# Four channels beside each other instead of two in the state of an FFT convolution

## The chip, the cores and the metric

The kernel runs on one core of one Trainium2 chip. The metric is the device time of one execution in microseconds; the time before is the median of three runs.

## The reference

A Hyena filter (a long convolution over the sequence) is followed by a feed-forward block with a cosine gate. Cut to what matters:

```python
# x, v: (4, 12480, 128); pos_emb: (12480, 64); w1: (64, 64); w2: (64, 128)
h_filt = (np.maximum(pos_emb @ w1, 0.0) @ w2) * np.exp(-0.01 * pos)[:, None]
u = x * v
L = 2 * S
Uf = np.fft.rfft(u, n=L, axis=1)
Hf = np.fft.rfft(h_filt, n=L, axis=0)
y = np.fft.irfft(Uf * Hf[None], n=L, axis=1)[:, :S]
x = (x * y).reshape(B * S, D)              # 49920 tokens of 128
h = x @ w_in                               # w_in: (128, 2048)
out = (h * np.cos(h)) @ w_out              # w_out: (2048, 128)
```

All of it is float32.

## The kernel before

The convolution is done by transforms written as matmuls. The sequence of one batch is seen as a grid of N1 = 96 by N2 = 120, and four transforms follow one another, each over one of the two sides of the grid:

- `f1` (lines 413 to 446 and 576): for each pair of channels, one matmul for each channel with the channel's data as weights (`u[:, b, 0:KE, i]`) and the table `c1` as the moving operand (192 columns).
- `f2` (449 to 483): for each of 96 frequencies, the table `w` as weights and the state of all 128 channels as the moving operand, 256 columns (real and imaginary part). `f2_product` multiplies with the filter's spectrum `h` on VectorE and adds on GpSimd.
- `i1` (485 to 498): again one channel at a time, the channel's data as weights, table `cs` as the moving operand (120 columns).
- `i2` (500 to 521): for each of 120 positions, a table `tm` as weights and the state of all channels as the moving operand (128 columns). The result times `x` goes to DRAM as rows for the feed-forward block.

The state between the transforms lies in one SBUF tile, `slots`, and every transform writes its result back into it. The 128 channels are 64 pairs: index `b` counts the pairs (`CB` = 64), index `i` the two of a pair. In each partition `slots` has, for each pair, 240 places with the two floats of the pair beside each other:

```python
slots = spool.tile([P, CB, 2 * N2, 2], F32, name="slots")
parts = slots[:, :, 0:2 * N1, :].rearrange("p b (r k) i -> p r k b i", r=2)
above = slots[:, :, 2 * N1:2 * N2, :]
```

So a transform that reads all channels at one place (f2, i2) takes pieces of two floats, 8 bytes, 1920 bytes apart. A transform that reads one channel (f1, i1) takes single floats 8 bytes apart. A step that writes one pair (the evictions of f1 and i1) writes a contiguous row. `ftile` holds the filter in the same manner, with 144 places for a pair (pieces 1152 bytes apart).

The program first makes the filter (lines 314 to 376), transforms it and the first batch (`f1`, then `f2` of both together), and runs `i1` of the first batch. In this first part (up to 348 us) a matmul is issued over all its weight columns at once. From `i2` of the first batch on, the convolution is issued beside the feed-forward block: a loop over blocks of tokens and 16 chunks of the hidden width issues one chunk at a time and takes as many steps of the convolution with it as a count of steps owed says. `tiled[0]` is then set, and `mm` (line 129) issues each matmul as two: one for output rows 0 to 63, one for the rest, each with its own weights and with the same moving operand. The order on every engine is the order of the program text; nothing is scheduled by costs.

In the feed-forward block a chunk is an up-projection (`ph`, 512 columns), the gate on ScalarE and VectorE, sums on GpSimd, and down-projections (`acca`, `accb`, 128 columns, line 787). Each batch passes f1, f2, i1 and i2 in turn; `i2` of one batch runs together with the loads and products of the next (`u_sums`, line 406).

Of the kernel before, what the change touches and what calls it, by code (L numbers as in the profile page):

```python
# [17 lines left out]
P = 128  # L18
# [15 lines left out]
def kernel(  # L34
# [62 lines left out]
    KF = N1 - 2 * (N2 - N1)  # L97
    CB = D // 2
    assert R * N2 == S and S + TAPS - 1 <= 2 * M and math.exp(DECAY * TAPS) < 2.0 ** -150
    assert D == P and DFF % P == 0 and FO * 2 == P and N1 % 2 == 0 and R <= P  # L100
# [11 lines left out]
    dram = ctx.enter_context(tc.tile_pool(name="dram", bufs=1, space=DRAM))  # L112
    hd = dram.tile([N1 // 2, N2, 2, CB, 4], F32, name="hd")
    zd = dram.tile([NROWS, G, D], F32, name="zd")
# [240 lines left out]
    def filter_hidden(bank, aT, i, peT, w1_sb):  # L355

        pa = bank()
        nc.tensor.matmul(pa[:, 0:ROWS * H], w1_sb[:, :], peT[:, :], start=True, stop=True)
        nc.scalar.activation(aT[:, 0:H, i * ROWS:(i + 1) * ROWS],
                             pa[:, 0:ROWS * H].rearrange("p (n a) -> p a n", a=H), AF.Relu)  # L360

    def filter_out(pool, bank, aT, slots, j, w2_sb):

        ps = bank()
        for i, jj in enumerate((j, H - 1 - j)):
            nc.tensor.matmul(ps[0:FR, i * 2 * D:(i + 1) * 2 * D], aT[:, jj, 0:FR],
                             w2_sb[:, :], start=True, stop=True)
        above = pool.tile([FR, 2, CB, 2], F32, name="above", bufs=2)
        pj = ps[0:FR, :].rearrange("p (n b i) -> p n b i", n=4, i=2)
        nc.scalar.copy(out=above[:, :, :, :], in_=pj[:, 2:4])  # L370
        a = H - 2 - 2 * j
        for place, op in ((a, ALU.add), (ODD + a, ALU.subtract)):
            nc.vector.tensor_tensor(
                slots[0:FR, :, place:place + 2, :].transpose([0, 2, 1, 3]),
                pj[:, 1::-1], above[:, :, :, :], op=op)
# [14 lines left out]
    def clear_gap(u):  # L390

        nc.gpsimd.memset(u[:, :, H:ODD, :], 0.0)

# [12 lines left out]
    def u_sums(u, tiles, a, takers):  # L406
        both = tiles[0][:, :, :].rearrange("p h (n b i) -> p h n b i", n=UA, i=2)
        below, above = both[:, 0, ::-1, :, :], both[:, 1, :, :, :]
        for place, op, e in ((a, ALU.add, takers[0]), (ODD + a, ALU.subtract, takers[1])):
            e.tensor_tensor(u[0:R, :, place:place + UA, :].transpose([0, 2, 1, 3]),  # L410
                            below, above, op=op)


    def f1_mm(ps, u, b, i):

        mm(ps[0:KE, i * 2 * N1:(i + 1) * 2 * N1], u[:, b, 0:KE, i],
           c1[0:u.shape[0], :, :].rearrange("p r k -> p (r k)"))
# [10 lines left out]
    def f1_evict(ps, b, share):  # L428
        copy, negated = f1_takers(b, share)
        pj = ps[:, 0:4 * N1].rearrange("p (i r k) -> p r k i", i=2, r=2)  # L430
        copy(out=parts[0:ODD, :, :, b, :], in_=pj[0:ODD])  # L431
        yield
        copy(out=parts[ODD:KE, 0, :, b, :], in_=pj[ODD:KE, 1])  # L433
        negated(parts[ODD:KE, 1, :, b, :], pj[ODD:KE, 0])
        yield

    def f1_evict_filter(ps, b, share):

        copy, negated = f1_takers(b, share)
        pj = ps[:, 0:4 * N1].rearrange("p (i k) -> p k i", i=2)  # L440
        near, far = ftile[:, b, :, :], above[:, b, :, :]
        copy(out=near[0:ODD], in_=pj[0:ODD, 0:N1 + KF])
        copy(out=far[0:ODD], in_=pj[0:ODD, N1 + KF:])
        yield
        copy(out=near[ODD:KE, 0:N1], in_=pj[ODD:KE, N1:])
        negated(near[ODD:KE, N1:], pj[ODD:KE, 0:KF])
        negated(far[ODD:KE], pj[ODD:KE, KF:N1])
        yield

    def f2_mm(ps, w, k1, i, filt=False):  # L450


        k = k1 + i
        pi = ps[0:N2, :].rearrange("p (r b g i) -> p g r b i", r=2, g=2, i=2)[:, i]
        if not filt:
            mm(pi, w[:, i, :], parts[0:KE, :, k])
        elif k < KF:
            both = ftile[0:KE, :, k:k + N1 + 1:N1, :].rearrange("p b r i -> p r b i")
            nc.tensor.matmul(pi, w[:, i, :], both, start=True, stop=True)
        else:  # L460
            for r, src in enumerate((ftile[0:KE, :, k, :], above[0:KE, :, k - KF, :])):
                nc.tensor.matmul(pi[:, r], w[:, i, :], src, start=True, stop=True)

    def f2_product(pool, ps, h, k1, whole):


        y = parts[0:N2, :, k1:k1 + 2, :, :].rearrange("p r k b i -> p r b (k i)")
        t = pool.tile([N2, 2, CB, 4], F32, name="t", bufs=2)
        uu = ps[0:N2, :].rearrange("p (r b j) -> p r b j", r=2, j=4)
        if whole:  # L470
            for r, (dst, hh) in enumerate(((y, h[:, :, :, :]), (t[:, :, :, :], h[:, ::-1, :, :]))):
                u = uu[:, r]
                twice = bass.AP(tensor=u.tensor, offset=u.offset,
                                ap=[u.ap[0], [0, 2], *u.ap[1:]])
                nc.vector.tensor_tensor(dst, twice, hh, op=ALU.mult)
                yield
        for r, op in ((0, ALU.subtract), (1, ALU.add)):
            if not whole:
                nc.vector.tensor_tensor(y[:, r], uu[:, 0], h[:, r], op=ALU.mult)
                yield  # L480
                nc.vector.tensor_tensor(t[:, r], uu[:, 1], h[:, 1 - r], op=ALU.mult)  # L481
            nc.gpsimd.tensor_tensor(y[:, r], y[:, r], t[:, r], op=op)  # L482
            yield

    def i1_mm(ps, b, i):
        for r in range(2):
            n = max(N1, CB + CB // 2 + 1) if tiled[0] else N1
            mm(ps[0:n, (i * 2 + r) * N2:(i * 2 + r + 1) * N2],
               slots[0:N2, b, r * N1:r * N1 + n, i], cs[:, r, :])

    def i1_evict(pool, ps, b):
# [3 lines left out]
        for h, op in ((0, ALU.add), (1, ALU.subtract)):  # L495
            nc.vector.tensor_tensor(slots[0:N1, b, h * N2:(h + 1) * N2, :], pj[:, 0],
                                    other[:, :, :], op=op)
            yield

    def i2_mm(ps, t, g, part):  # L500
        for i in range(part * G // 2, (part + 1) * G // 2):
# [8 lines left out]
            for r, place in enumerate(places):  # L510
                mm(ps[0:R, i * D:(i + 1) * D], t[:, i, r, :], slots[0:N1, :, place, :],
                   start=(r == 0), stop=(r == 1))
# [83 lines left out]
    def f2_units(bank):  # L596
        with tc.tile_pool(name="there", bufs=3) as pool:
            ws, hs = {}, {}

            def before(j):  # L600
                ws[j] = pool.tile([KE, 2, N2], F32, name="w")
                nc.sync.dma_start(ws[j][:, :, :], wd[j, :, :, :])
                hs[j] = pool.tile([N2, 2, CB, 4], F32, name="h")
                nc.sync.dma_start(hs[j][:, :, :, :], hd[j, :, :, :, :])
# [10 lines left out]
    def f2_both_units(bank):  # L615

        with tc.tile_pool(name="both", bufs=2) as pool:
# [15 lines left out]
            def after(j, ps):  # L633
                h = pool.tile([N2, 2, CB, 4], F32, name="h", bufs=3)
                nc.scalar.activation(h[:, :, :, :].rearrange("p r b j -> p (r b j)"),
                                     ps[1][0:N2, :], AF.Copy, scale=1.0 / M)
# [58 lines left out]
    def inverse_units(bank, b):  # L695
# [3 lines left out]
        if b + 1 == B:  # L699
            yield from i2_units(bank, b, 3)  # L700
            return
        new = u_units(b + 1, 3, slots[0:R, :, :, :],
                      lambda j, half: nc.vector if half else nc.gpsimd,
# [9 lines left out]
    def forward_units(bank, back):  # L713

        f2 = f2_units(bank)
        next(f2)
        yield from f1_units(bank, slots[0:R, :, :, :])
        yield from f2
# [116 lines left out]
    with tc.manual_schedule():  # L835
        with tc.tile_pool(name="psum", bufs=8, space=PSUM) as psum, \
# [4 lines left out]
            spool = ctx.enter_context(tc.tile_pool(name="slots", bufs=1))  # L841
            slots = spool.tile([P, CB, 2 * N2, 2], F32, name="slots")
            parts = slots[:, :, 0:2 * N1, :].rearrange("p b (r k) i -> p r k b i", r=2)
            above = slots[:, :, 2 * N1:2 * N2, :]
            aT = above.rearrange("p b j i -> p b (j i)")

# [4 lines left out]
            with tc.tile_pool(name="layers", bufs=1, side="right") as pool:  # L851
# [8 lines left out]
                for i in range(1, NCH):  # L860
                    pes[i] = filter_load(pool, i)
                first_u = u_units(0, 3, slots[0:R, :, :, :],
                                  lambda j, half: nc.vector if half and j % 3 and j < 18
# [4 lines left out]
                window = filter_window(pool)  # L868
                nc.gpsimd.memset(aT[:, 0:H, NCH * ROWS:FR], 0.0)
                sines = forward_tables(pool)  # L870
# [15 lines left out]
            fpool = first.enter_context(tc.tile_pool(name="ftile", bufs=1, side="right"))  # L886
            ftile = fpool.tile([P, CB, N1 + KF, 2], F32, name="ftile")
            clear_gap(ftile[0:FR, :, :, :])
            with tc.tile_pool(name="out", bufs=1, side="right") as pool:
                for j in range(H // 2):  # L890
                    filter_out(pool, bank, aT, ftile, j, w2_sb)
                    for _ in range(1 + (j % 3 == 0)):
                        next(first_u)
            f1 = f1_units(bank, ftile[0:FR, :, :, :], 0.53, f1_evict_filter)
            for _ in first_u:
# [15 lines left out]
            def beside(units, pieces, factor, more=lambda pool: iter(())):  # L911
                with tc.tile_pool(name="convert", bufs=1) as pool:
# [8 lines left out]

            beside(f1_units(bank, slots[0:R, :, :, :], 0.55),
                   [(wind[:, c], w) for c, w in in_pieces], INV_TWO_PI)
# [124 lines left out]
```

## Time and profile before

| what | value |
|---|---|
| median of 3 runs | 3749.4 us (3748.94 to 3753.12) |
| profiled execution | 3748.55 us |
| its span, first to last instruction | 3746.8 us |
| mean granted TensorE clock | 0.994 |
| TensorE busy | 97% of the span |
| GpSimd, VectorE, ScalarE busy | 74%, 79%, 60% |

PE is TensorE's matmuls, PEld its weight loads, DVE VectorE, ACT ScalarE, POOL GpSimd. Each float32 matmul stands in the trace as two records. A name such as `cv<-slots,tm` says that `cv` (a PSUM tile; `ps` in the first part) is written from `slots` and `tm`; `96*64 96x128` is 96 rows by 64 columns of weights and a moving operand of 128 columns. The stages in the trace, from the first to the last matmul of each:

| batch | f1 | f2 | i1 | i2 |
|---|---|---|---|---|
| first, with the filter | 75 to 177 | 181 to 279 | 282 to 343 | 348 to 583 |
| second | 612 to 748 | 753 to 1084 | 1093 to 1201 | 1202 to 1424 |
| third | 1452 to 1586 | 1593 to 1921 | 1933 to 2074 | 2078 to 2300 |
| fourth | 2327 to 2464 | 2470 to 2798 | 2809 to 2950 | 2955 to 3089 |

After 3089 us only the feed-forward block is left.

### The profile page before, as it was taken

How to read it: one execution, taken by the hardware profiler on the slowest of the kernel's cores; microseconds unless marked ns; L12 is line 12 of the kernel's file. 1: busy time of each engine (PE TensorE's matmuls, PEld its weight loads, DVE VectorE, ACT ScalarE, POOL GpSimd, SP SyncE). 2: the span in 40 equal slices, each digit the busy share in tenths (PEclk: the TensorE clock that was granted, in tenths of full speed). 3: DMA queues.
4: the chain of work that ended last, by engine and by line, in shares of the span. 5: the costliest groups of instructions: out<-in, count | busy, mean ns of one | idle time of the engine just before them, and what ended most of it. 6: DMA issues, size and time to landing. Idle time of an engine off the chain costs nothing.

```text
span 3746.8 us, 101339 instructions
## 1 busy us (share of the span) xinstructions
PE 3631.1 (97%) x40298; PEld 2592.9 (69%) x40298; DVE 2962.2 (79%) x5812; ACT 2252.4 (60%) x4660; POOL 2786.1 (74%) x3271
## 2 busy tenths in 40 slices
PE   7898999999999999999999999999999999999999
PEld 6777776766668776666667776766667776666666
DVE  7887887788887777788877777788887667777777
ACT  5756666655554556655555555665555446666666
POOL 6667887588874887588874788578884447887877
PEclk9999999999999999999999999999999999999999
DMA  6263551022212661022210553012220350000000
GB/s 167 66 185 100 163 155 49 20 65 72 73 43 58 169 163 45 18 69 73 66 40 21 157 163 99 15 53 73 67 70 13 107 147 21 21 19 24 18 24 14
DMA packets 209710, 279.59 MB, mean 75 GB/s; under 512 B 17112, under 2 KB 146536, under 8 KB 209112
## 3 DMA queue, kind: packets, MB, share of 16 engines
q1 hardware_dynamic: 209239, 273.12, 25.7%
q8 instruction: 320, 5.24, 0.6%
q14 instruction: 151, 1.23, 0.1%
HBM read 193.64 MB, written 79.42 MB: 73 GB/s over the span
## 4 chain that ended last, share of the span: by engine, by line
PE 79%; DVE 7%; POOL 2%; ACT 2%; issue 1%; DMA 0%; ACTq 0%; SPq 0%; POOLq 0%; DVEq 0%
PE ph L132 28%; PE cv L132 20%; PE accb L787 16%; PE acca L787 12%; DVE gt L762 2%; DVE gt L756 2%; PE cv L136 1%; ACT gt L755 1%; PE ph L136 1%; POOL ts L770 1%; DVE slots L431 0%; ACT tile L818 0%; POOL slots L410 0%; POOL ts L773 0%; DVE slots L433 0%
## 5 line engine op out<-in xcount | busy, mean ns | idle before, releaser
L755 ACT ACTIVATE gt<-ph 128x512 int32<-128x512 f32 (+1 forms) x1374 | 818.5, 596 | 1175.2 <-PE ph L132 1123.3
L756 DVE SCALAR_TENSOR_TENSOR gt<-ph,gt 128x512 f32<-128x512 f32 (+1 forms) x1374 | 944.3, 687 | 676.8 <-ACT gt L755 666.8
L770 POOL TENSOR_TENSOR ts<-gt 128x512 f32<-128x512 f32 (+2 forms) x784 | 1005.0, 1282 | 608.7 <-PE accb L787 542.1
L132 PE MATMUL ph<-at,w_in_sb 128*64 128x512 f32 (+1 forms) x5496 | 1428.6, 593 | 26.6 <-ACT tile L818 17.0
L761 ACT ACTIVATE gt<-gt 128x512 f32<-128x512 f32 (+1 forms) x1568 | 972.2, 620 | 4.2 <-DVE gt L756 3.4
L762 DVE TENSOR_TENSOR gt<-ph,gt 128x512 f32<-128x512 f32 (+1 forms) x1374 | 932.3, 679 | 0.0
L787 PE MATMUL accb<-ts,w_out_sb 128*64 128x128 f32 (+2 forms) x9408 | 652.2, 272 | 0.0
L774 POOL TENSOR_TENSOR ts<-gt,ts 128x256 f32<-128x256 f32 (+2 forms) x784 | 574.3, 733 | 61.5
L773 POOL TENSOR_TENSOR ts<-ts,gt 128x256 f32<-128x256 f32 (+2 forms) x784 | 573.0, 731 | 61.5
L787 PEld LDWEIGHTS acca<-gt,w_out_sb 128*64 128x64 f32 x6272 | 404.5, 137 | 239.1 <-issue 200.2
L787 PEld LDWEIGHTS accb<-ts,w_out_sb 128*64 128x64 f32 x9408 | 546.1, 137 | 0.0
L787 PE MATMUL acca<-gt,w_out_sb 128*64 128x128 f32 (+2 forms) x6272 | 482.9, 272 | 0.0
L787 PEld LDWEIGHTS accb<-gt,w_out_sb 128*64 128x64 f32 x3136 | 230.1, 137 | 254.8 <-issue 198.3
L132 PEld LDWEIGHTS ph<-at,w_in_sb 128*64 128x64 f32 x5496 | 354.9, 137 | 51.3 <-ACT tile L818 22.4
L482 POOL TENSOR_TENSOR slots<-slots,t 120x256 f32<-120x256 f32 x384 | 281.3, 739 | 125.8 <-DVE t L481 81.3
L132 PEld LDWEIGHTS cv<-slots,tm 96*64 96x64 f32 (+1 forms) x3840 | 246.6, 128 | 129.0 <-issue 118.3
L787 PE MATMUL accb<-gt,w_out_sb 128*64 128x128 f32 (+1 forms) x3136 | 313.6, 273 | 5.1 <-DVE ot L808 3.3
L787 PE MATMUL acca<-ts,w_out_sb 128*64 128x128 f32 (+1 forms) x3136 | 311.6, 272 | 2.3 <-POOL ts L773 2.3
L132 PE MATMUL cv<-slots,tm 96*64 96x128 f32 (+1 forms) x3840 | 278.7, 287 | 7.4 <-POOL tm L306 5.6
L132 PEld LDWEIGHTS cv<-cs,slots 120*64 120x64 f32 (+1 forms) x3072 | 167.3, 125 | 80.3 <-issue 70.9
L787 PEld LDWEIGHTS acca<-ts,w_out_sb 128*64 128x64 f32 x3136 | 204.8, 137 | 3.1 <-POOL ts L773 2.8
L132 PEld LDWEIGHTS cv<-c,slots 104*64 104x64 f32 (+1 forms) x1536 | 118.3, 137 | 114.6 <-issue 63.6
(145 smaller groups left out, 4134.9 us busy)
## 6 DMA issues: line engine op xcount, KB each, us to landing
h<-hd SPq DMA_DIRECT2D x144, 240.0 KB
tm<-td SPq DMA_DIRECT2D x96, 312.0 KB
xt<-in_x_dram SPq DMA_DIRECT2D x120, 208.0 KB
vt<-in_v_dram SPq DMA_DIRECT2D x120, 208.0 KB
xs<-in_x_dram SPq DMA_DIRECT2D x120, 208.0 KB
zd<-xs SPq DMA_DIRECT2D x119, 208.0 KB
tile<-zd SPq DMA_DIRECT2D x96, 256.0 KB
w<-wd SPq DMA_DIRECT2D x144, 116.2 KB
```

The costliest lines, as they stand in the source:

```text
L132: nc.tensor.matmul(dst[lo:hi], left[:, lo:hi], right, start=start, stop=stop)
L136: nc.tensor.transpose(dst, src, ident[0:n, 0:n])
L482: nc.gpsimd.tensor_tensor(y[:, r], y[:, r], t[:, r], op=op)
L755: nc.scalar.activation(turns, ph[:, 0:m], AF.Identity, bias=phase)
L756: nc.vector.scalar_tensor_tensor(out=part, in0=ph[:, 0:m], scalar=phase, in1=turns, op0=ALU.add, op1=ALU.subtract)
L761: nc.scalar.activation(part, part, AF.Sin, scale=scale)
L762: nc.vector.tensor_tensor(part, ph, part, op=ALU.mult)
L770: nc.gpsimd.tensor_tensor(ts[:, 0:2, 0:half], gt[:, :, half:2 * half], gt[:, 0, 0:2 * half].rearrange("p (h n) -> p h n", h=2), op=ALU.sub ...
L773: nc.gpsimd.tensor_tensor(t[2], t[1], b11, op=ALU.add)
L774: nc.gpsimd.tensor_tensor(t[3], b21, t[2], op=ALU.subtract)
L787: nc.tensor.matmul(acc[h * CB:(h + 1) * CB, place, 0:r], w_out_sb[:, pair, weight, :], right[:, h * r:(h + 1) * r], start=(pair == 0 and i ...
```

## The change

The 64 pairs become 32 groups of four channels. `slots` gets the shape (128, 32, 240, 2, 2): a place holds the four floats of a group beside each other, `e` saying which pair of the group and `i` which of the pair, and channel pair `b` is now group `b // 2`, `e = b % 2`. All views follow. A transform that reads all channels at one place takes pieces of four floats, 16 bytes, 3840 bytes apart; one that reads one channel takes single floats 16 bytes apart; an eviction of one pair writes pieces of two floats at a pitch of 16 bytes. `ftile`, the filter's hidden layer `aT`, the spectrum `h` in DRAM (`hd`) and the product's term `t` are laid out in the same way. Each instruction computes on the same elements as before; only their addresses differ. The slots tile starts at a multiple of 16 bytes in both.

```diff
+    Q = CB // 2
-    hd = dram.tile([N1 // 2, N2, 2, CB, 4], F32, name="hd")
+    hd = dram.tile([N1 // 2, N2, 2, Q, 8], F32, name="hd")
...
 def u_sums(u, tiles, a, takers):
-            e.tensor_tensor(u[0:R, :, place:place + UA, :].transpose([0, 2, 1, 3]),
+            e.tensor_tensor(u[0:R, :, place:place + UA].rearrange("p c n e i -> p n c (e i)"),
                             below, above, op=op)
 def f1_mm(ps, u, b, i):
-        mm(ps[0:KE, i * 2 * N1:(i + 1) * 2 * N1], u[:, b, 0:KE, i],
+        mm(ps[0:KE, i * 2 * N1:(i + 1) * 2 * N1], u[:, b // 2, 0:KE, b % 2, i],
            c1[0:u.shape[0], :, :].rearrange("p r k -> p (r k)"))
 def f1_evict(ps, b, share):
-        copy(out=parts[0:ODD, :, :, b, :], in_=pj[0:ODD])
+        copy(out=parts[0:ODD, :, :, b // 2, b % 2, :], in_=pj[0:ODD])
...
 def f2_mm(ps, w, k1, i, filt=False):
-        pi = ps[0:N2, :].rearrange("p (r b g i) -> p g r b i", r=2, g=2, i=2)[:, i]
+        pi = ps[0:N2, :].rearrange("p (r c g j) -> p g r c j", r=2, g=2, j=4)[:, i]
-            mm(pi, w[:, i, :], parts[0:KE, :, k])
+            mm(pi, w[:, i, :], parts[0:KE, :, k].rearrange("p r c e i -> p r c (e i)"))
...
 def f2_product(pool, ps, h, k1, whole):
-        y = parts[0:N2, :, k1:k1 + 2, :, :].rearrange("p r k b i -> p r b (k i)")
-        t = pool.tile([N2, 2, CB, 4], F32, name="t", bufs=2)
+        y = parts[0:N2, :, k1:k1 + 2].rearrange("p r k c e i -> p r c (k e i)")
+        t = pool.tile([N2, 2, Q, 8], F32, name="t", bufs=2)
 def i1_mm(ps, b, i):
-               slots[0:N2, b, r * N1:r * N1 + n, i], cs[:, r, :])
+               slots[0:N2, b // 2, r * N1:r * N1 + n, b % 2, i], cs[:, r, :])
 def i1_evict(pool, ps, b):
-            nc.vector.tensor_tensor(slots[0:N1, b, h * N2:(h + 1) * N2, :], pj[:, 0],
+            nc.vector.tensor_tensor(slots[0:N1, b // 2, h * N2:(h + 1) * N2, b % 2, :], pj[:, 0],
                                     other[:, :, :], op=op)
 def i2_mm(ps, t, g, part):
-                mm(ps[0:R, i * D:(i + 1) * D], t[:, i, r, :], slots[0:N1, :, place, :],
+                mm(ps[0:R, i * D:(i + 1) * D], t[:, i, r, :], slots[0:N1, :, place].rearrange("p c e i -> p c (e i)"),
                    start=(r == 0), stop=(r == 1))
...
-            slots = spool.tile([P, CB, 2 * N2, 2], F32, name="slots")
-            parts = slots[:, :, 0:2 * N1, :].rearrange("p b (r k) i -> p r k b i", r=2)
+            slots = spool.tile([P, Q, 2 * N2, 2, 2], F32, name="slots")
+            parts = slots[:, :, 0:2 * N1].rearrange("p c (r k) e i -> p r k c e i", r=2)
```

## The prediction

> **What bounds the kernel now.** I read the busy shares first: TensorE is busy for 97% of the span. Since that may be a mean over stages with different limits, I then took the busy time of each engine by stage, with the borders at the first and last matmul of each stage of the convolution.
>
> ```profile
> PE 3631.1 (97%) x40298; PEld 2592.9 (69%) x40298; DVE 2962.2 (79%) x5812; ACT 2252.4 (60%) x4660; POOL 2786.1 (74%) x3271
> ```
>
> Columns by stage: window, its length, busy time of PE, PEld, DVE, ACT and POOL, granted clock, DMA share, GB/s.
>
> ```profile
> 75.50:176.60 101.10, 86.81 (x488) 81.73 (x487) 86.08 (x264) 79.92 (x283) 68.32 (x108) 0.95 0.24 71
> 282.30:343.10 60.80, 49.79 (x462) 46.95 (x462) 50.55 (x143) 40.19 (x124) 47.36 (x59) 0.92 0.21 62
> 348.10:582.90 234.80, 226.19 (x2752) 166.13 (x2750) 196.95 (x353) 158.27 (x336) 205.81 (x254) 0.99 0.53 155
> 1592.70:1920.90 328.20, 318.77 (x3337) 205.71 (x3336) 278.93 (x552) 192.91 (x352) 286.54 (x337) 1.00 0.24 69
> 1932.90:2074.10 141.20, 139.63 (x1960) 108.44 (x1956) 108.13 (x236) 75.59 (x173) 69.81 (x77) 1.00 0.07 20
> 2078.00:2300.00 222.00, 221.04 (x2706) 163.83 (x2704) 163.31 (x277) 117.95 (x216) 193.03 (x228) 1.00 0.60 163
> ```
>
> In order: the first transform of the filter and of batch 0, the third transform of batch 0, its fourth beside the feed-forward block, and second, third and fourth transform of a later batch. In the last three PE is busy for 97 to 99.6%, and the chain of waits there runs almost wholly over PE: what a matmul gains or loses goes into the span. In the first two PE has gaps.
>
> The third view is the timeline of PE, for the spacing from one group's start to the next group's. A pair is one record for each half of the columns, running side by side.
>
> ```profile
> 1596.29 0.65 PE L132 MATMUL cv<-slots,w 124*64 124x256 f32 x4
> 1596.75 0.41 PE L787 MATMUL accb<-gt,w_out_sb 128*64 128x128 f32 x4
> ...
> 2010.07 1.40 PE L132 MATMUL cv<-cs,slots 120*64 120x120 f32 x24
> 2011.30 0.61 PE L787 MATMUL acca<-gt,w_out_sb 128*64 128x128 f32 x8
> ...
> 2203.97 1.15 PE L132 MATMUL cv<-slots,tm 96*64 96x128 f32 x16
> 2204.94 0.62 PE L787 MATMUL acca<-gt,w_out_sb 128*64 128x128 f32 x8
> 2205.38 0.41 PE L787 MATMUL acca<-ts,w_out_sb 128*64 128x128 f32 x4
> ```
>
> The fourth transform takes 0.97/8 = 121 ns per pair of 128 columns where the feed-forward pair, with contiguous operands, takes 0.44/4 = 110. Over all groups of the trace the fourth transform has 122.5; the second has 243 per pair of 256 columns (230 in the group shown) where half of a contiguous 512-column pair (0.86/2, the ph groups) is 215. The third transform is at 1.23/12 = 102.5 for 120 columns: full rate. So there is an excess of 10 to 13%, only where the moving operand is read in pieces of 8 bytes and two halves run side by side: the second transform undivided (batch 0) has 218.
>
> The fourth view is the weight loads by shape; the mean is the second number behind the bar.
>
> ```profile
> L132 PEld LDWEIGHTS cv<-slots,tm 96*40 96x40 f32 x1920 | 223.9, 117 | 22.0 <-issue 22.0
> L132 PEld LDWEIGHTS cv<-cs,slots 120*64 120x64 f32 x1536 | 167.1, 138 | 78.8 <-issue 69.5 <-ACT ot L801 4.7 <-DVE slots L496 4.2
> L132 PEld LDWEIGHTS cv<-cs,slots 120*33 120x33 f32 x1536 | 159.2, 111 | 1.4 <-issue 1.4
> L366 PEld LDWEIGHTS ps<-w_sb,slots 128*96 128x96 f32 x120 | 19.5, 163 | 7.7 <-POOL ftile L392 1.5
> L462 PEld LDWEIGHTS ps<-slots,w 124*120 124x120 f32 x96 | 14.0, 180 | 0.0
> ```
>
> From 33 to 64 columns a load grows by 27 ns, 0.85 per column (40 to 64 from contiguous weights: 0.86; 96 contiguous: 163), so I read it as a fixed 84 ns, which the next matmul does not wait out (spacing 102.5, load 138), and 0.833 per column. Loads of slots read one float in two (8-byte pitch) at about the same rate; undivided they take 167 (96 columns) and 193 (124) at the median, 4 and 9 ns over the line.
>
> **The change, part by part.** Engine by engine both programs have the same instructions in the same order with the same waits; DMAs move the same contiguous 2 KB per partition. Only access patterns differ.
>
> *Removed: the 8-byte pieces of moving operands.* [...] I take the excess as gone but for a little: 12 of 12.5 ns on 1920 pairs (fourth) and 25 of 28 on 576 (second). In full for three batches of the fourth: 1440 x 12 = 17.3 us. Half for batch 0, where PE is at 96% and POOL at 88%: 480 x 6 = 2.9. 85% of the second transform's 14.4, since its chain runs over DVE for some 10%: 12.2. Sum -32 us; bounds 0 (the excess comes from two streams whatever the piece) and -42 (1920 x 13.5 + 576 x 28). Undivided there is nothing to regain (218 against 216).
>
> *Added: weights at a pitch of 16 bytes* in the first and third transforms. No row has it. One bound is nothing: the pitch went from 4 to 8 bytes for at most 9 ns. [...] If a fetch costs 1.67 ns whether it gives one column or two, a column costs 1.67. I take this, as nearest to the last rows. Then:
> - third transform, divided: 64 columns load in 107 ns, with some 3 for the hand-over 110 against 102.5. The first pair of each group of 8 or 12 loads under a long matmul, so 0.9 x 1536 x 7.5 = +10 us.
> - third, undivided: 96 columns, 160 + 2.5 against 102.6. 512 records x 162.5 = 83 us in a stage of 60.8, where PE had 52.5 and gaps that mostly close as it becomes the bound: stage 85, +24.
> - first, undivided: 124 columns, 209 against 163. 256 records each for filter and batch 0: 53.5 us in stretches of 49.5 and 51.6; 56 and 55 with what gaps stay: +10.
> - first, divided: 107 ns lie under 160 of matmul: 0. If the cover were gone it would cost 768 pairs by the difference.
> Sum +44, bounds 0 and +87 (13% more on each load, as the moving streams have it: divided third 124, +29; undivided +35 and +23).
>
> [...]
>
> *Moved: evictions write 8-byte pieces at a 16-byte pitch* where they wrote whole rows (L431, L433, L442 to L445, L425, L496). On DVE the row L373 writes 256 floats so in 411 ns, L479 in longer pieces in 415: 0. ACT has no such row: 0, at most 4 us (13% of the 31 us of batch 0's evictions). POOL's sums (L410, 758 ns) may near the 733 of contiguous L773: off the path, 0. L482 (739) stays.
>
> Sum: +44 - 32 = +12 us on the profiled execution of 3748.55 (span 3746.8 and 1.75 around it), 3760.6. It lies 0.85 below the median of 3749.4, so 3761.4 on that scale.
>
> **Rivals.**
> *Free weights.* A single float per fetch still comes every 0.833 ns. Then only the gain is left: -32, 3717. For: 8 bytes cost next to nothing, divided loads 1 ns. Against: the 4 and 9 ns and the excess. [...]
> *Loads that take turns.* With a fetch per column the loads of both halves share what is there: 97 columns x 1.67 = 162 for the third transform, 0.9 x 1536 x 59 = +82; 124 x 1.67 = 207 against 166 for the first, 0.9 x 768 x 41 = +28; with the undivided +34 and -32: +112, 3861. It decides from the point where a load's share passes 102.5 ns. For: the excess appears only with two streams. Against: for the last block of rows (88 columns) pairs are 76 ns apart with 64 + 64 columns loaded, so contiguous loads run side by side.
> *No gain.* The excess stays at 16 bytes, now at hops of 3840 bytes: +44, 3793. Against: contiguous streams side by side have none.
>
> **How the numbers follow.** My forecast has 0.45, with a range of its own from -7 (gain 40, cost 33) to +38 (gain 25, cost 63): 3742 to 3787. Free weights 0.30, turns 0.15, no gain 0.10. About 0.2%, 7.5 us, is what a measurement here can tell. Faster: 0.29 of free weights and 0.05 of the forecast, 0.34. Within: 0.12 and 0.01. Slower: 0.28, 0.15 and 0.10, 0.53. The range leaves out most of "turns" and a little of either end: low -38, high +76 (cost 87, a third of the gain).
>
> **What would show it.** Loads of 64 columns from slots near 190 ns, of 96 near 244, of 124 near 290; third-transform pairs near 110, undivided 162; the fourth near 110 and the second near 218; batch 0's third transform near 85 us. Loads still at 138 show free weights; third pairs near 160 with divided loads over 230, turns; fourth pairs at 122, no gain. Wrong altogether would be a stage that grows on ACT or DVE with PE's spacing unchanged.

## The result, and the profile after

| what | before | after |
|---|---|---|
| median | 3749.17 us (3747.57 to 3753.12, 4 runs) | 3781.49 us (3780.69 to 3783.34, 4 runs) |
| span of the profiled execution | 3746.8 us | 3780.4 us |

The ratio is 1.0086, 95% interval 1.0070 to 1.0102: slower by 32 us. The forecast was 3761.4, with a range of 3711 to 3825.

Busy shares of the whole program after, from the top of the page:

```profile
PE 3680.1 (97%) x40298; PEld 2708.4 (72%) x40298; DVE 2997.5 (79%) x5812; ACT 2264.1 (60%) x4660; POOL 2777.7 (73%) x3271
```

The same instructions, and PE still at 97%: 49 us more of matmul in a span that is 34 us longer. This view can't say which matmuls. The windows by stage can: window, length, busy time of PE, PEld, DVE, ACT and POOL, clock, DMA share, GB/s. They are, in order, the first transform of the filter and of batch 0, the third and the fourth of batch 0, then the second, third and fourth of the third batch, each from its first to its last matmul.

```profile
64.70:124.10 59.40, 59.39 (x257) 59.40 (x257) 49.78 (x164) 40.12 (x173) 47.91 (x88) 0.96 0.31 87
124.10:182.30 58.20, 58.15 (x257) 57.90 (x256) 42.18 (x116) 42.52 (x122) 29.48 (x32) 1.00 0.19 53
285.80:377.20 91.40, 91.29 (x512) 90.92 (x512) 51.85 (x150) 44.15 (x127) 45.23 (x59) 0.98 0.18 56
379.10:610.10 231.00, 219.92 (x2697) 159.58 (x2699) 193.95 (x343) 154.21 (x331) 201.10 (x247) 0.97 0.55 161
1620.60:1945.00 324.40, 316.55 (x3366) 208.22 (x3364) 276.96 (x548) 193.35 (x353) 282.90 (x333) 1.00 0.24 68
1956.90:2105.30 148.40, 146.69 (x1971) 129.42 (x1969) 111.06 (x239) 76.78 (x175) 70.05 (x77) 1.00 0.07 18
2109.20:2325.50 216.30, 215.08 (x2728) 162.45 (x2726) 171.85 (x272) 115.22 (x212) 185.57 (x223) 1.00 0.61 168
```

The windows in the prediction, and the stage table ahead of it, are read from the trace's own zero, which lies 11 us before the first instruction, while these views count from the first instruction. So the lengths given there are those of the stages, but the busy times belong to stretches that begin 11 us late. Batch 0's third transform before, with its own borders, holds all of its 512 records:

```profile
271.30:332.10 60.80, 56.01 (x512) 54.56 (x512) 45.34 (x140) 38.72 (x120) 41.95 (x55) 0.97 0.27 84
```

PE was busy there for 92% of the time, and not for 82%. The prediction's sums go by lengths and by the spacing of matmuls, and do not change.

Two signs at once. The stages that read moving pieces became shorter (fourth transform 234.8 to 231.0 and 222.0 to 216.3, second 328.2 to 324.4). The stages that load weights from the state became longer, and in the first part PEld now runs for nearly as long as PE (90.92 of 91.29 us, before 54.56 of 56.01): loads are what PE waits for there. All stages together:

| stages | change, us |
|---|---|
| fourth transform, four batches | -3.8, -5.6, -5.6, -6.3 = -21.4 |
| second transform, later three batches | -12.6 |
| third, divided, later three batches | +7.6, +7.2, +7.2 = +22.0 |
| third, undivided, batch 0 | +30.6 |
| first, undivided, filter and batch 0 | +9.8, +6.6 = +16.4 |
| first, divided, later three batches | +3.4 |
| between the stages of the first part | about -5 |

That is -34 and some +72, less 5: +33 of the 33.6 us by which the span grew.

Weight loads by shape (the second number behind the bar is the mean in ns). The first two lines are the undivided loads before:

```profile
L132 PEld LDWEIGHTS ps<-cs,slots 120*96 120x96 f32 x512 | 54.6, 171 | 9.2 <-POOL slots L482 3.7 <-ACT some L300 2.7 <-ACT spare L305 1.8
L132 PEld LDWEIGHTS ps<-c,slots 104*124 104x124 f32 x256 | 43.3, 199 | 8.2 <-ACT slots L423 8.1
...
L133 PEld LDWEIGHTS cv<-cs,slots 120*64 120x64 f32 x1536 | 204.4, 211 | 24.5 <-issue 12.9 <-ACT ot L803 3.6 <-DVE slots L498 3.1
L133 PEld LDWEIGHTS cv<-cs,slots 120*33 120x33 f32 x1536 | 162.4, 144 | 19.3 <-issue 0.4
L133 PEld LDWEIGHTS cv<-c,slots 104*64 104x64 f32 x768 | 132.6, 196 | 96.6 <-issue 50.8 <-PE cv L133 21.7 <-ACT slots L425 12.0
L133 PEld LDWEIGHTS ps<-cs,slots 120*96 120x96 f32 x512 | 91.0, 273 | 3.5 <-POOL slots L484 3.5
L133 PEld LDWEIGHTS ps<-c,slots 104*124 104x124 f32 x256 | 58.1, 323 | 0.0
```

A load of 33 columns has a median of 138, one of 64 has 193 where a long matmul covers it: 1.78 ns for each further column, where before (111 and 138) it was 0.87. Where the load is what PE waits for (third transform, undivided loads) it shows some 23 ns more: 216, 273 and 323 for 64, 96 and 124 columns, again 1.78 for each further column.

The timeline of PE: undivided first and third transform, then the second, third and fourth of a later batch with what follows each:

```profile
149.67 2.66 PE L133 MATMUL ps<-c,slots 104*124 104x192 f32 x11
...
299.80 4.40 PE L133 MATMUL ps<-cs,slots 120*96 120x120 f32 x24
...
1637.24 0.63 PE L133 MATMUL cv<-slots,w 124*64 124x256 f32 x4
1637.67 0.63 PE L789 MATMUL acca<-gt,w_out_sb 128*64 128x128 f32 x8
...
2042.07 1.61 PE L133 MATMUL cv<-cs,slots 120*33 120x120 f32 x23
2043.42 0.30 PE L789 MATMUL acca<-gt,w_out_sb 128*64 128x128 f32 x1
2043.52 0.28 PE L133 MATMUL cv<-cs,slots 120*64 120x120 f32 x1
2043.56 0.57 PE L789 MATMUL acca<-gt,w_out_sb 128*64 128x128 f32 x6
...
2246.94 1.07 PE L133 MATMUL cv<-slots,tm 96*64 96x128 f32 x16
2247.81 0.64 PE L789 MATMUL acca<-gt,w_out_sb 128*64 128x128 f32 x8
```

- Undivided: 24 records of the third in 4.40 us, less one of about 0.3 at the end, are 177 ns apart (it was 102.6); 11 of the first in 2.66, less 0.4, are 227 apart (it was 163).
- Second: 0.43/2 = 215 per pair, over all groups 218 (243 before).
- Third, divided: the half with 33 columns is done after 1.35 us, the half with 64 after 1.49, against 1.23 for both before. The records show the two halves out of step: the feed-forward block begins in one half while the other still works on the transform. Over the stage a pair costs 117 (102.5 before); the loads of 64 follow one another at 120.
- Fourth: 0.87/8 = 109, over all groups 110 (122.5 before).

The three spacings at which PE waits for loads, 120, 177 and 227 ns for 64, 96 and 124 columns, lie on one line: 1.78 ns per column and 6 more. (The expectations below have 1.70, which takes the prediction's 84 ns for the fixed part of a load.)

### The profile page after: what moved, and what is told of

It is laid out like the page before. It is cut to its first block, busy times and chain, and to the rows that moved or that the text cites. A ratio compares the mean times of both kernels' runs of the same rounds, so it can differ in the third digit from the quotient of the medians.

```text
span 3780.4 us, 101339 instructions
## 1 busy us (share of the span) xinstructions
PE 3680.1 (97%) x40298; PEld 2708.4 (72%) x40298; DVE 2997.5 (79%) x5812; ACT 2264.1 (60%) x4660; POOL 2777.7 (73%) x3271
## 3 DMA queue, kind: packets, MB, share of 16 engines
q14 instruction: 150, 1.23, 0.1%
## 4 chain that ended last, share of the span: by engine, by line
PE 78%; DVE 7%; ACT 2%; issue 1%; POOL 1%; DMA 0%; ACTq 0%; DVEq 0%; POOLq 0%; SPq 0%
PE ph L133 28%; PE cv L133 20%; PE accb L789 16%; PE acca L789 12%; DVE gt L764 2%; DVE gt L758 2%; PE cv L137 1%; ACT gt L757 1%; PE ph L137 1%; ACT tile L820 0%; DVE t L483 0%; POOL ts L772 0%; DVE ot L810 0%; DVE xt L406 0%; DVE ot L807 0%
## 5 line engine op out<-in xcount | busy, mean ns | idle before, releaser
L133 PE MATMUL ph<-at,w_in_sb 128*64 128x512 f32 (+1 forms) x5496 | 1450.2, 593 | 27.7 <-ACT tile L820 17.0
L789 PE MATMUL accb<-ts,w_out_sb 128*64 128x128 f32 (+2 forms) x9408 | 666.0, 272 | 0.0
L789 PE MATMUL acca<-gt,w_out_sb 128*64 128x128 f32 (+2 forms) x6272 | 496.8, 272 | 0.0
L133 PEld LDWEIGHTS ph<-at,w_in_sb 128*64 128x64 f32 x5496 | 368.9, 137 | 52.5 <-ACT tile L820 22.5
L789 PE MATMUL accb<-gt,w_out_sb 128*64 128x128 f32 (+1 forms) x3136 | 329.1, 274 | 5.4 <-DVE ot L810 4.1
L789 PE MATMUL acca<-ts,w_out_sb 128*64 128x128 f32 (+1 forms) x3136 | 323.0, 272 | 2.9 <-POOL ts L775 2.7
L133 PEld LDWEIGHTS cv<-slots,tm 96*40 96x40 f32 (+1 forms) x3840 | 229.5, 128 | 124.4 <-issue 114.4
L133 PEld LDWEIGHTS cv<-cs,slots 120*33 120x33 f32 (+1 forms) x3072 | 232.3, 178 | 43.8 <-issue 13.2
L133 PE MATMUL cv<-slots,tm 96*40 96x128 f32 (+1 forms) x3840 | 255.8, 275 | 4.7 <-POOL tm L307 2.5
L133 PE MATMUL cv<-cs,slots 120*33 120x120 f32 (+1 forms) x3072 | 223.5, 278 | 0.0
```

What stands on the lines that cost most here:

```text
L133: nc.tensor.matmul(dst[lo:hi], left[:, lo:hi], right, start=start, stop=stop)
L789: nc.tensor.matmul(acc[h * CB:(h + 1) * CB, place, 0:r], w_out_sb[:, pair, weight, :], right[:, h * r:(h + 1) * r], start=(pair == 0 and i ...
```

## Experiments

**e4_pitch: the weights' pitch alone.** The kernel before, with the third transform's weights read every second place:

```diff
-               slots[0:N2, b, r * N1:r * N1 + n, i], cs[:, r, :])
+               slots[0:N2, b, r * 46:r * 46 + 2 * n:2, i], cs[:, r, :])
```

> The kernel before, with one thing changed: the third transform reads its weights from every second place of its own row (16 bytes from column to column in place of 8), so it computes on the wrong places; evictions, the moving operands and all else are those of before. Theory of the load: loads of 64 columns 193 to 216 ns, of 96 columns 273; spacing 120 and 177; the third transform's stages grow by 30 us in the first part and by some 7.3 us in each of three later batches: 3749 + 52 = 3801. Rival 'evictions': 3749, no change.

3799.3 us (3797.35 to 3801.14), ratio 1.0131 (1.0115 to 1.0146). Evictions, moving operands and everything else are those of before. Its loads by shape:

```profile
L132 PEld LDWEIGHTS cv<-cs,slots 120*64 120x64 f32 x1536 | 203.8, 210 | 23.6 <-issue 12.4 <-ACT ot L801 3.3 <-DVE slots L496 2.8
L132 PEld LDWEIGHTS ps<-cs,slots 120*96 120x96 f32 x512 | 90.7, 273 | 3.9 <-POOL slots L482 3.9
```

The loads of the changed kernel to 1 ns, and its stages: 90.9, 115.6, 148.3 and 148.5 us against 91.4, 115.7, 148.4 and 148.6. So what the third transform lost is the pitch of its weights, and the evictions that now write broken rows have no part in it.

**e2_split: one load, or two side by side.** The changed kernel, with first and third transform of the first part issued in two halves of the columns, as in the later batches:

```diff
+    def halves(dst, left, right):
+        was, tiled[0] = tiled[0], True
+        mm(dst, left, right)
+        tiled[0] = was
...
-            mm(ps[0:n, (i * 2 + r) * N2:(i * 2 + r + 1) * N2],
+            halves(ps[0:n, (i * 2 + r) * N2:(i * 2 + r + 1) * N2],
```

(`f1_mm` likewise, and `n` as for divided columns.)

> The changed kernel, with the first and third transform of the first part issued in two halves of the columns (0 to 63 and the rest), as they are issued later beside the feed-forward block. Theory (a column of weights at a pitch of 16 bytes takes 1.70 ns, the halves load side by side, and a matmul waits for its load): the largest load of the first part is 64 columns, 193 ns in place of 323 and 273; the first transform's spacing is 163 again (load 109 under 160 of matmul), its two stretches 49 to 52 us in place of 59.2 and 58.3; the third transform's spacing is 120 in place of 177, its stage some 68 us in place of 91.4. Together -40 us: about 3742. Rival 'evictions' (the time goes into writes of 8-byte pieces by ScalarE and VectorE): within 4 us of the changed kernel's 3781. Rival 'turns' (loads of both halves share one stream of fetches): no gain either, spacing stays at 165 or more for the third transform and above 205 for the first.

3743.76 us (3742.24 to 3745.7), ratio 0.9984 (0.9975 to 0.9992): 38 us less than the changed kernel, and a little under the kernel before. The third transform of batch 0 went from 91.4 to 65.0 us, the two stretches of the first from 117 to 103. Its loads there:

```profile
L133 PEld LDWEIGHTS ps<-cs,slots 120*64 120x64 f32 x512 | 61.7, 216 | 0.1
L133 PEld LDWEIGHTS ps<-c,slots 104*64 104x64 f32 x256 | 42.3, 196 | 10.1 <-ACT slots L430 10.1
L133 PEld LDWEIGHTS ps<-c,slots 104*60 104x60 f32 x256 | 42.1, 188 | 1.2
```

Two loads, of 64 and 33 columns, run at the same time: the third transform is at 120 here, where loads in turns would need over 160, and the first is back at 163. "Loads that take turns" falls, and the loss in the first part is shown to hang on the issue as much as on the layout: 41 of its 47 us were the undivided loads.

**e5_ladder: what a load counts.** The kernel before, with weights of another pitch in each batch (4-byte floats: 20 bytes undivided in batch 0, then 12, 4 and 8 bytes):

```diff
+        pitch = (5, 3, 1, 2)[turn_of[0]]
+        flat = slots[0:N2, b, :, :].rearrange("p j i -> p (j i)")
...
+        return flat[:, at:at + pitch * (n - 1) + 1:pitch]
```

> The kernel before with another pitch of the third transform's weights in each batch (all inside the pair's own row, so on wrong places): batch 0, undivided, 20 bytes; batch 1, halves, 12 bytes; batch 2 4 bytes; batch 3 8 bytes as before. Durations of the loads are read, not the total. Theory 'one fetch of 1.70 ns for each 16 bytes touched': at 12 bytes four columns touch three such lines, 1.28 ns a column: 64 columns 84 + 82 = 166 ns, spacing still at 103; at 20 bytes 1.70 as at 16: 96 columns near 273; at 4 and 8 bytes 137 to 138. Rival 'threshold' (any step over 8 bytes takes a fetch of its own): 12 bytes like 16, 193 to 216 ns and a spacing of 118 to 120. [...]

3773.82 us (one run). The loads at 20, 12 and 4 bytes, most of each stage's:

```profile
L132 PEld LDWEIGHTS ps<-cs,slots 120*96 120x96 f32 x448 | 75.1, 262 | 0.0
L132 PEld LDWEIGHTS cv<-cs,slots 120*64 120x64 f32 x465 | 51.2, 165 | 14.5 <-issue 12.0 <-ACT ot L810 1.2 <-DVE slots L504 1.0
L132 PEld LDWEIGHTS cv<-cs,slots 120*64 120x64 f32 x464 | 50.7, 136 | 27.8 <-issue 24.3 <-ACT ot L810 1.8 <-DVE slots L504 1.6
```

At 12 bytes four columns lie in three lines of 16 bytes, as the expectation counts them. By the covered loads at 16 bytes (79 ns and 1.78 per line) that gives 79 + 64 x 0.75 x 1.78 = 164, measured 165, and 123 for 33 columns, measured 123. At 4 and at 8 bytes (136 and 138) two or more columns share a line, and the loads are as fast as before. So up to 16 bytes these loads cost, beyond some 80 ns, 1.78 ns for each line of 16 bytes that they touch, or 0.87 per column, whichever is more. A line is only the unit of this count: the count fits these times, and what the memory does was not shown. At 20 bytes a column is a little cheaper than at 16 (262 against 273 ns for 96 columns, spacing 167 against 177), though it touches as many lines; why stays open.

**e8_gain: the gain without the cost.** The changed kernel with halves as in e2, and the third transform's weights read from a constant table at 8 bytes' pitch:

```diff
+               even[0:N2, :, :].rearrange("p a k -> p (a k)")[:, i:i + 2 * n - 1:2], cs[:, r, :])
```

> The changed kernel without its slow loads: the third transform takes its weights at a pitch of 8 bytes from a constant table (so its results are not the transform's), and the first transform of the first part is issued in halves, so that its loads lie under its matmuls. Only the gain of the 16-byte moving pieces is left. Theory: second and fourth transform as in the changed kernel (218 and 110 per pair), third at 102.5: 3749 - 34 + 3 = 3718. Rival 'evictions': the broken writes are still there, so only what the loads cost goes, 3760 to 3781. If the gain of the moving operands hung on the slower third transform (work shifted between stages), less than half of the 34 would be left: above 3732.

3722.55 us (3721.19 to 3725.0), ratio 0.9928 (0.9915 to 0.9940). The third transform's loads are back:

```profile
L133 PEld LDWEIGHTS cv<-cs,even 120*64 120x64 f32 x1536 | 167.1, 138 | 80.3 <-issue 70.9 <-ACT ot L808 4.7 <-DVE slots L503 4.2
```

Its pairs are at 102.5 again, and the fourth transform stays at 216.2 us. That is -27 us, with some +3 left in each part of the first transform. Second and fourth transform alone are 33 us shorter than before, by the lengths of their stages.

**e7_thirds: three narrower tiles.** The changed kernel with halves in the first transform, and the third issued as three tiles of 32 columns, so that each load has half as many columns:

```diff
+            for lo in range(0, N1, N1 // 3):
+                nc.tensor.matmul(
+                    ps[lo:lo + N1 // 3, (i * 2 + r) * N2:(i * 2 + r + 1) * N2],
+                    slots[0:N2, b // 2, r * N1 + lo:r * N1 + lo + N1 // 3, b % 2, i],
+                    cs[:, r, :], start=True, stop=True)
```

> A version that may beat both: the changed kernel with the third transform always issued in three column tiles of 32 and the first transform of the first part in halves. Theory: a load of 32 columns takes 54 ns of fetches (138 in all), under the 100 ns of the matmul, if three tiles load side by side; spacing 102.5, the gain of 34 stays: about 3715. Rival 'two streams only' (three tiles' fetches get in each other's way, as two moving streams of 8-byte pieces did by 13%): loads above 150 and spacing 115 or more, 3740 to 3770. Rival 'issue': six instructions for 100 ns are too many for PE's queue, spacing above 110 with loads at 138.

3763.13 us (3757.32 to 3764.05), ratio 1.0032 (1.0020 to 1.0045): a miss by 48 us. The loads did what was expected, as the first row says, and the stage did not (the second row is the window of the third batch's third transform, columns as above; the rest is PE around one group):

```profile
L495 PEld LDWEIGHTS cv<-cs,slots 120*32 120x32 f32 x4608 | 157.8, 138 | 111.0 <-issue 98.0 <-DVE slots L505 6.5 <-ACT ot L810 6.5
1922.30:2078.30 156.00, 154.88 (x2480) 104.09 (x2480) 108.73 (x239) 76.81 (x176) 69.99 (x77) 1.00 0.06 17
...
2036.55 1.03 PE L133 MATMUL ph<-at,w_in_sb 128*64 128x512 f32 x4
2037.51 1.46 PE L495 MATMUL cv<-cs,slots 120*32 120x120 f32 x36
2038.90 0.66 PE L796 MATMUL acca<-gt,w_out_sb 128*64 128x128 f32 x8
2039.39 0.39 PE L796 MATMUL acca<-ts,w_out_sb 128*64 128x128 f32 x4
```

Within a group the tiles follow at 102.5, and the first part, where nothing else lies between them, has 63.9 us. Beside the feed-forward block each change between tiles of 64 and of 32 columns costs time: in the rows above the `ph` matmuls take 0.96 us to the next group where two pairs took 0.86, the 12 triples 1.39 instead of 1.23, the four pairs behind them 0.49 instead of 0.44. The later stages are 9.5, 14.8 and 14.8 us longer than before, 39 together, and e8, which has no such changes and whose loads stay hidden too, is 40.6 us faster. With some 52 groups in a stage, 14.8 us are 0.28 per group, for two changes.

**e6_moving, e9_hops, e10_orders: why 8-byte pieces were slow.** The prediction took the size of the piece for the cause. Three kernels vary the fourth transform's reads in the last batch of the kernel before. e6: ten groups with pieces of 16 bytes on a border of 16, ten with such pieces 8 bytes off it, ten with 8-byte pieces, all even pairs and then all odd:

```diff
+        if g >= 20:
+            return slots[0:N1, :, place, :].rearrange("p (c e) i -> p e c i", e=2)
+        at = place - place % 2 if g < 10 else min(place - place % 2 + 1, 2 * N2 - 3)
+        return slots[0:N1, ::2, at:at + 2, :].rearrange("p c n i -> p c (n i)")
```

> The kernel before, with the fourth transform of the last batch reading its moving operand in three ways, ten groups each (on wrong places in the first twenty): groups 0 to 9 in pieces of 16 bytes on 16-byte borders, 32 of them 3840 bytes apart; 10 to 19 the same pieces starting 8 bytes behind a border; 20 to 29 in pieces of 8 bytes, but first every even pair and then every odd one, 3840 bytes apart. The weights are those of before. Theory (two streams get in each other's way by the number of 16-byte lines that they touch): 109 to 110 per pair, then 122, then 122. Rival 'length of the piece' (four floats beside each other are enough wherever they start): 110, 110, 122. Rival 'hop' (1920 bytes is a bad distance, 3840 a good one): 110 in all three.

3752.25 us (one run). The three readings in the timeline, in that order:

```profile
2965.13 1.95 PE L132 MATMUL cv<-slots,tm 96*64 96x128 f32 x32
2966.88 0.64 PE L795 MATMUL acca<-gt,w_out_sb 128*64 128x128 f32 x8
...
3013.24 1.21 PE L132 MATMUL cv<-slots,tm 96*64 96x128 f32 x16
3014.27 0.61 PE L795 MATMUL acca<-gt,w_out_sb 128*64 128x128 f32 x8
...
3070.70 1.34 PE L132 MATMUL cv<-slots,tm 96*64 96x128 f32 x16
3071.87 0.61 PE L795 MATMUL acca<-gt,w_out_sb 128*64 128x128 f32 x8
```

1.75/16 = 109 on the border, 1.03/8 = 129 off it (127 over its groups), 1.17/8 = 146 for the last (141 over its groups). The last has the same pieces and touches as many lines as the order of before, at 122: a count of lines doesn't give it. So e9 varied the distance of 8-byte pieces alone (`hop`, in floats):

```diff
+        hop = (480, 482, 484, 476, 472, 464, 448)[min(g // 4, 6)]
+        at = slots[0:N1, 0, place % 64, :]
+        return bass.AP(tensor=at.tensor, offset=at.offset, ap=[at.ap[0], [hop, CB], [1, 2]])
```

> The kernel before, with the fourth transform of the last batch reading 64 pieces of 8 bytes at another distance in each four groups (on wrong places): 1920 bytes as before, then 1928, 1936, 1904, 1888, 1856, and 1792 in the last six. It asks why 8-byte pieces 3840 bytes apart took 141 ns per pair and 1920 apart 122. Theory (only the number of 16-byte lines counts): 122 at every distance. Rival 'banks' (the distance decides which streams meet): 1920 and 1792 (15 and 14 times 128) at 122 or more, some of the others at 109 to 112; then rows padded to such a distance would give the gain of the change without its slow weights.

3754.32 us (one run). Two of its readings, 1936 and 1888 bytes:

```profile
2993.77 2.00 PE L132 MATMUL cv<-slots,tm 96*64 96x128 f32 x32
2995.61 0.39 PE L794 MATMUL accb<-gt,w_out_sb 128*64 128x128 f32 x4
...
3028.31 1.46 PE L132 MATMUL cv<-slots,tm 96*64 96x128 f32 x16
3029.60 0.62 PE L794 MATMUL acca<-gt,w_out_sb 128*64 128x128 f32 x8
```

| distance, bytes | 1792 | 1856 | 1888 | 1904 | 1920 | 1928 | 1936 | 3840 (e6) |
|---|---|---|---|---|---|---|---|---|
| ns per pair | 144 | 113 | 160 | 117 | 122 | 122 | 115 | 141 |

The same pieces, in as many lines, go from 113 to 160 by their distance, while one stream alone had almost none at 1920 bytes (218 for 256 columns, 215 contiguous; other distances were not tried with one stream). Why the distance counts was not shown. e10 left the layout alone and changed the order in which the 64 pairs are read, in steps of 1, 4, 8, 16 and 32 pairs, six groups each:

```diff
+                e = (1, 4, 8, 16, 32)[g // 6] if b + 1 == B else 1
+                if e > 1:
+                    to = to.rearrange("p (c e i) -> p e c i", e=e, i=2)
+                    what = what.rearrange("p (c e) i -> p e c i", e=e)
```

> The kernel before, same places, same rows; only the order in which the fourth transform of the last batch takes the 64 pairs is another (and the order in which it writes PSUM, so the results are the same): groups 0 to 5 one after the other (1920 bytes), then 6 groups each in steps of 4, 8, 16 and 32 pairs (7680, 15360, 30720 and 61440 bytes). Rival 'banks', which the distances of 1856 to 1936 bytes spoke for (113 to 160 ns): some order comes near 110, others go beyond 122. Theory of lines alone: 122 throughout. Should PSUM written in pieces of 8 bytes cost time of its own, all four lie above 122.

3748.09 us (one run): 122, about 118 (114 to 138 in single groups), about 121, 126 and 114. The last of them:

```profile
3070.19 1.08 PE L132 MATMUL cv<-slots,tm 96*64 96x128 f32 x16
3071.09 0.40 PE L791 MATMUL accb<-gt,w_out_sb 128*64 128x128 f32 x4
```

0.90/8 = 113: with `e=32` pair b is followed by the pair 32 behind it, and most of the excess is gone with the old layout as it was. The results go to PSUM in the same new order, so this run changes reading and writing together; e6 and e9 changed the reading alone.

**e12_order, e13_both, e11_pad: the gain on the old layout.** e12 is the kernel before with `e = 32` in the fourth transform of every batch; e13 has it in the second transform too, issued as two matmuls of 128 columns:

```diff
+            for r in range(2):
+                mm(pi[:, r].rearrange("p (c e) i -> p e c i", e=32), w[:, i, :],
+                   parts[0:KE, r, k].rearrange("p (c e) i -> p e c i", e=32))
```

> A version that may beat both, in the layout of before: the fourth transform of every batch takes the pairs in the order b, b + 32 (0, 32, 1, 33 and so on), which the last run showed at 114 per pair in place of 122. Theory (the excess is two streams meeting, and the distance decides): 1920 x 8 ns, less a part in batch 0: 12 to 15 us, 3735 to 3738; weights and evictions as before. Rival 'lines': 3750.

> [...] Theory: the second transform goes from 243 to 2 x 114 = 228 per 256 columns, 576 x 15 = 9 us, of which 85% counts: 3727 to 3731. Rival: writing PSUM by parts or the second load of the same weights eats it, 3736 and more.

e12: 3734.87 us (3733.28 to 3738.92), ratio 0.9963 (0.9949 to 0.9977). e13: 3729.82 us (3726.91 to 3730.96), ratio 0.9945 (0.9932 to 0.9957): e8 aside, which leaves work out, the fastest here, 21 us under the kernel before and 52 under the changed one. Both as expected. The timeline of e13, fourth and second transform:

```profile
2203.93 1.09 PE L132 MATMUL cv<-slots,tm 96*64 96x128 f32 x16
2204.84 0.41 PE L793 MATMUL accb<-gt,w_out_sb 128*64 128x128 f32 x4
...
1604.73 0.65 PE L132 MATMUL cv<-slots,w 124*64 124x128 f32 x8
1605.19 0.41 PE L793 MATMUL accb<-gt,w_out_sb 128*64 128x128 f32 x4
```

0.91/8 = 114, and 0.46/4 = 115 for each half of a second-transform pair, 231 in all over its groups (243 before).

e11 is the kernel before with two unused places in each row, so that pieces lie 1936 bytes apart. To make room, the filter's `above` has one buffer, and the table `cs` is loaded later:

```diff
-            slots = spool.tile([P, CB, 2 * N2, 2], F32, name="slots")
+            slots = spool.tile([P, CB, 2 * N2 + 2, 2], F32, name="slots")
```

> The layout of before with two unused places behind each pair's row, so that pairs stand 1936 bytes apart (115 to 116 per pair in the run over distances); for the space the filter's last step has one buffer in place of two and the third transform's table is loaded after the second transform of batch 0. Theory: 1920 x 6.5 ns in the fourth transform, 12 us less a part in batch 0; the second transform from 243 towards 230, some 6 us; the two things done for space cost 2 to 8 us in the first part: 3735 to 3742. Rival 'lines': 3752 to 3758.

3740.66 us (3738.15 to 3741.69), ratio 0.9971 (0.9962 to 0.9981). Pairs are at 116 in the fourth and 229 in the second transform, as e9's 115 said, and these stages are 20 us shorter. The two things done for space cost 10 of them: the first part starts its first transform 6.4 us later than before and its third 9.9 us later.

## Why the prediction was right, and where its sum was off

The direction and both of its parts held: slower, because a weight load at 16 bytes' pitch takes 1.78 ns for each further column where it took 0.87 (193 against 138 ns for 64 columns), while the moving side gains what it was given. That the time lies in the range says little by itself, since the range reached from 38 us faster to 76 slower; the time grew by 32 us where 12 were forecast. Step by step:

- *The gain*: -34 us against -32. Fourth transform 110 per pair as predicted, second 218; -21.4 and -12.6 against -20.2 and -12.2. Batch 0's fourth gave back 3.8 (2.9 predicted). That pieces of 16 bytes would do nearly as well as a contiguous row was assumed; e6 shows it for pieces on a border of 16 (109 per pair, 110 contiguous) and not for the same pieces 8 bytes off it (127).
- *One fetch per column*: near as a time. No run shows a fetch, or the 1.67 ns put for it; the runs show 1.78 ns for each further column at 16 bytes, and 2 x 0.87 = 1.74 for two columns at 8. The few ns of excess at 8 bytes, which the prediction held against free weights, did stand just before a rise: in e5 64 columns took 136 ns at 4 bytes, 138 at 8 and 165 at 12.
- *The spacing where PE waits for a load* was the term that was mis-sized: 110, 162.5 and 211.5 were put for 64, 96 and 124 columns, and 120, 177 and 227 were measured. The 0.11 ns per column make 7, 11 and 14 ns of that; the hand-over, put at 3 and 2.5, is some 6. This gives third divided +22 against +10, third undivided +30.6 against +24, first undivided +16.4 against +10, together 25 us short. The border gaps that closed give 5 back.
- *First, divided*, at 0: the spacing stayed at 163 under the longer loads, but the stages grew by 3.4 us. In each of them 15 to 19 pairs stood 188 ns before the next; after, 21 to 25 stand 245 before it, 55 more, as a load of 64 columns takes 193 instead of 138. These gaps sum to 3.8 us more than before, which fits loads that no matmul covers; no run tests it.
- With the gain's 2, that is 25 + 3 - 5 - 2 = 21 us, about the difference between the forecast and the measured growth.
- *Evictions* at 0: nearly. ScalarE's 64x384 copy (L431, now L433) went from 458 to 500 ns; every run that has its broken writes has the first transform's slow loads too, so the two are not told apart. VectorE's row of the third transform (L496, now L498) went from 395 to 415 ns, but not by the writes alone: e8 and e7 have the same writes and 396, e4 has the slow loads with contiguous writes and 395. What the two together do to it stays open. VectorE's copy of the first transform stayed at 540 to 541. None of it sets the third transform: e4, with contiguous evictions, has the same stages. GpSimd's sums stayed (758 to 755).

The rivals: *free weights* is refuted by e4 and e5: 64 columns took 136 to 216 ns by pitch and by what covered them. *Turns* is refuted by e2. *No gain* is refuted by e8.

One reason behind a right term was wrong. The excess of the 8-byte pieces in the moving streams was held against free weights, too, as if it came from the size of the piece. e9 shows that two such streams have it by their distance, 113 to 160 at the same bytes and lines, and e12 and e13 take most of it away without touching the layout. Why was not shown. That weights at 16 bytes came out slow is luck as far as it was expected from this excess.

## What to carry to other kernels

When a layout makes one operand of a matmul contiguous, price the other one: weights 16 bytes from column to column took 1.78 ns for each further column here, where they had taken 0.87 at 8 bytes. That was nearly free only where the matmuls follow one another more slowly than the loads can (163 ns in the divided first transform against 1.78 x 64 + 6 = 120: +3.4 us over three batches); the third, at 102.5, paid 22.0. The loads of a matmul's two halves ran side by side (e2: 120 per pair, where loads in turns would need over 160), so dividing took away 41 of the 47 us that the first part had lost. Before a layout is changed for a slow stream, try another order of reading it: here that alone gave 21 us, about two thirds of the gain, and no other stage got longer by more than about 1 us.

## What was not expected of the hardware

- Two streams of 8-byte pieces side by side take 113 to 160 ns per pair by their distance: 1856 and 1888 bytes are 32 bytes and 47 ns apart.
- A change between tiles of 64 and of 32 columns costs about 0.14 us of PE (e7: 0.28 per group of the third transform, for two changes): two of them are twice the 0.14 us (10 pairs x 14.5 ns) that the shorter loads save in a group.
- A pitch of 20 bytes loads a little faster than one of 16 (262 against 273 ns for 96 columns, e5 and e4).
- The halves of a divided matmul run out of step where their loads are the bound, by some 0.14 us per group of twelve (1.35 against 1.49 us).
